# A two-level Winograd MLP on one core: one SBUF pool placed by a search over buffer times, w1 in quarter blocks, layer norm of the second half on two engines

## The chip, the core and the metric

The kernel runs on one core of a Trainium2 chip. The core has a matrix engine (TensorE, PE in the profile, with its weight loads as PEld), VectorE (DVE), ScalarE (ACT), GpSimd (POOL) and SyncE (SP), which here issues nearly all DMA transfers. Each engine executes its own instructions in order and waits for others through semaphores; SP's DMA instructions wait in the same way, so one that waits holds up those behind it. The metric is the device time of one execution in microseconds (us), as the median of several runs.

## The reference

```python
def _layernorm(x, axis=-1, eps=1e-5):
    m = jnp.mean(x, axis=axis, keepdims=True)
    v = jnp.var(x, axis=axis, keepdims=True)
    return (x - m) / jnp.sqrt(v + eps)

# x: 1 x 2048 x 1024, w1: 1024 x 3584, w2: 3584 x 1024, all bf16
def reference(x, w1, b1, w2, b2):
    y = _layernorm(x, axis=-1)
    h = _gelu(jnp.einsum("bsd,df->bsf", y, w1) + b1)
    return jnp.einsum("bsf,fd->bsd", h, w2) + b2
```

## The kernel before

**The two GEMMs.** The 2048 rows of x are two blocks of 1024 (b = 0, 1). Both GEMMs use Winograd's form of Strassen's algorithm, in which a 2 x 2 product of blocks takes 7 products instead of 8. The first GEMM has one level of it: an output group (b, r), r = 0 to 13, is computed in 7 *steps* q = 1 to 7 of 4 matmuls with 512 columns each (L880). Its operands are w1, in chunks of two groups, with four sums of each chunk (DVE, L747), and the normalized, transposed x (y) with three T sums (DVE, L696). The second GEMM has two levels: 7 outer products p, each for both blocks, each of 7 steps of 14 matmuls with 256 columns (L1133). Its operands are the gelu output h (A11 to A22, and their sums S1 to S4, L1048), inner sums of those (L1037), and "units" of W2: for product p and step q a unit of 448 KB is loaded by `w2_unit` from W2 itself (for q = 1, 2, 4 where the operand of p is a plain block of W2), from the scratch tensor w2_raw (q = 1, 2, 4 of the operands T1 to T4) or from w2_scr (the inner sums, q = 5, 6, 7, 3).

**Preparing W2.** Class `W2Sums` makes these scratch tensors while the first GEMM runs. It does so in slices of the 7 row tiles (0-2, 2-4, 4-6, 6-7), each of 14 lambdas in a row: loads of the blocks of W2 (L920), outer differences (L930), inner differences (L946), stores to w2_raw (L942) and w2_scr (L954). In each slice the sums of B11, which product 1 uses, come first, and those of T4, which product 4 uses, last. The temporaries lie in an allocator of their own, MZ, over a zone of 20 KB per partition at the end of the SBUF pool; buffers born before the first unit may not lie there.

**Around a group.** Class `Wino` combines the steps of a group in PSUM: ACT saves partial sums and copies banks (L806, L815), DVE adds (L823), ACT applies gelu (L799) in the first GEMM; in the second, DVE adds and finishes (L1065, L1078) and SP stores the output (L1057). Layer norm of a tile i of 128 rows is `norm(i)`: for tiles in `ACT_LN`, mean and variance by two ACT passes (L618, L621), else by two bn_stats and an aggregate on DVE (L635 to L638); then a power on POOL and the normalization on DVE. Tiles 8 to 15 (block 1) are all in `ACT_LN`. Their transposition is a DMA (L678).

**The order.** The program is written as a list of steps, `flat`. The opening and part of group rows 0 to 10 of block 0 lie ahead of it. Then come 53 steps for what is left of rows 0 to 10, 20 for rows 11 to 13, 98 for block 1 (from position `fB` = 73 on) and the steps of the second GEMM (from `fC` = 171 on), where a step of a group alternates with one of the group before. `put(i, f)` hangs other work on a position of this list. Such a position is the earliest one for DMAs: a load may not start before the PE step ahead of that position has ended (`gate`). A2_LA, A1_LA and UNIT_LA say how many steps ahead of its first use a load is placed, SUM_LA the same for the w1 sums, `W2_AT` from where to where a slice of W2 is spread ("A" counts from 0, "B" from fB), Y1_AT and Y1_STEP where the x tiles of block 1 go. Within these limits a list scheduler (`Program._simulate`) sets the order of instructions on each engine, by a latest start time (`alap`) that follows from the first PE step that needs the result. It runs on modelled durations: the PE order is fixed.

**The placement.** A first pass runs without limits of memory and gives each buffer a time of first use and of last use. Class `Plan` then gives each buffer its offset, largest area first, at the spot with the least lateness (`_pack`). The program is built again with these offsets; a buffer laid over an earlier one waits for that one's last users. This is repeated 6 times with learned times, and the order with the shortest modelled span is used.

**Sizes.** In bytes per partition, one h buffer (`h_unit`) has 7,168, and there are 4 x 2 of them in each block; a W2 unit has 3,584, a quarter of a w1 chunk 2,048, S1 of block 0 is 14,336 for itself.

## Time and profile before

| | us |
|---|---|
| runs of the kernel before, lowest / median / highest | 354.06 / 356.14 / 358.99 |
| the profiled execution | 357.63 |
| its span, first to last instruction | 355.9 |

The span is 1.7 us shorter than the profiled execution's own time. Times in profile rows are microseconds unless marked ns, counted from the start of the span. A row of a group of instructions has line, engine, operation, tiles, form and count, then busy time and mean ns of one, then the idle time of the engine ahead of them and what ended it. The last slices of the page's table of busy tenths belong to the second GEMM, which begins at about 190 us. The granted clock is the share of its full clock at which TensorE runs; 1.00 is full.

### The profile page before, as it was taken

How to read it: one execution, taken by the hardware profiler on the slowest of the kernel's cores; microseconds unless marked ns; L12 is line 12 of the kernel's file. 1: busy time of each engine (PE TensorE's matmuls, PEld its weight loads, DVE VectorE, ACT ScalarE, POOL GpSimd, SP SyncE). 2: the span in 40 equal slices, each digit the busy share in tenths (PEclk: the TensorE clock that was granted, in tenths of full speed). 3: DMA queues.
4: the chain of work that ended last, by engine and by line, in shares of the span. 5: the costliest groups of instructions: out<-in, count | busy, mean ns of one | idle time of the engine just before them, and what ended most of it. 6: DMA issues, size and time to landing. Idle time of an engine off the chain costs nothing.

```text
span 355.9 us, 6022 instructions
## 1 busy us (share of the span) xinstructions
PE 336.5 (95%) x2363; PEld 221.4 (62%) x2363; DVE 294.6 (83%) x465; ACT 187.2 (53%) x327; POOL 13.3 (4%) x32
## 2 busy tenths in 40 slices
PE   8899999979979999998996999999999999998995
PEld 6754443434424444443443778888888888886884
DVE  5976599986989769777999899969997897797964
ACT  2498999979957676674765433353111112211110
POOL 2210101001300000000000000000000000000000
PEclk9999999999999999999999899999999999999999
DMA  7961988999997799879996355373665737558552
GB/s 242 320 150 29 290 277 307 235 331 320 225 294 213 225 334 291 253 249 316 278 287 191 103 152 161 104 207 119 190 183 157 206 116 199 171 176 236 162 159 64
DMA packets 99157, 75.82 MB, mean 213 GB/s; under 512 B 11962, under 2 KB 90426, under 8 KB 99130
## 3 DMA queue, kind: packets, MB, share of 16 engines
q1 hardware_dynamic: 98986, 75.32, 72.0%
q8 instruction: 18, 0.29, 0.4%
q10 hardware_dynamic: 144, 0.13, 0.1%
q14 instruction: 9, 0.07, 0.1%
HBM read 48.96 MB, written 24.38 MB: 206 GB/s over the span
## 4 chain that ended last, share of the span: by engine, by line
PE 62%; DMA 23%; ACT 6%; DVE 5%; issue 3%; SPq 1%; DVEq 0%
PE ps L1133 34%; PE ps L880 26%; DMA mem<-in_w_dram 10%; DMA mem<-w_raw 7%; DMA mem<-in_x_dram 5%; ACT mem L799 2%; DVE mem L747 2%; ACT mem L815 2%; PE ps L1184 2%; DMA mem<-w_scr 1%; DVE ps L823 1%; PE ps L664 1%; DVE mem L946 1%; ACT mem L621 1%; DVE mem L696 1%
## 5 line engine op out<-in xcount | busy, mean ns | idle before, releaser
L880 PE MATMUL ps<-mem 128*128 128x512 f16 x756 | 167.6, 381 | 6.7 <-ACT mem L815 2.6
L1133 PE MATMUL ps<-mem 128*128 128x256 f16 (+1 forms) x1372 | 152.7, 273 | 7.3 <-DMA mem<-w_raw 4.2
L1133 PEld LDWEIGHTS ps<-mem 128*128 128x128 f16 x1372 | 133.8, 98 | 26.8 <-DMA mem<-w_raw 5.9
L880 PEld LDWEIGHTS ps<-mem 128*128 128x128 f16 (+1 forms) x756 | 72.5, 98 | 98.1 <-ACT mem L815 6.6
L815 ACT COPY mem<-ps 128x512 f32<-128x512 f32 x111 | 65.5, 595 | 82.4 <-PE ps L1133 69.9
L799 ACT ACTIVATE mem<-ps,b_sb 128x512 f16<-128x512 f32 x112 | 74.2, 705 | 22.7 <-DVE ps L823 13.6
L823 DVE TENSOR_TENSOR ps<-ps,mem 128x512 f32<-128x512 f32 x84 | 58.2, 693 | 19.1 <-ACT mem L815 14.2
L1037 DVE TENSOR_TENSOR mem<-mem 128x1792 f16<-128x1792 f16 x56 | 60.0, 1084 | 8.7 <-PE ps L1133 6.2
L946 DVE TENSOR_TENSOR mem<-mem 128x512 f16<-128x512 bf16 (+5 forms) x84 | 38.1, 464 | 10.5 <-DMA w_scr<-mem 6.9
L747 DVE TENSOR_TENSOR mem<-mem 128x1024 f16<-128x1024 bf16 (+1 forms) x56 | 37.0, 686 | 6.5 <-DMA mem<-in_w_dram 6.2
L806 ACT COPY ps<-ps 128x512 f32<-128x512 f32 x31 | 17.9, 576 | 34.7 <-PE ps L1133 31.0
L1048 DVE TENSOR_TENSOR mem<-mem 128x1792 f16<-128x1792 f16 x32 | 34.0, 1082 | 1.9 <-PE ps L1133 1.9
L1065 DVE TENSOR_TENSOR mem<-ps,mem 128x512 bf16<-128x512 f32 x24 | 16.3, 684 | 3.7 <-DMA out_dram<-mem 2.0
L930 DVE TENSOR_TENSOR mem<-mem 128x2048 f16<-128x2048 bf16 (+1 forms) x16 | 17.4, 1087 | 0.2
L1078 DVE TENSOR_TENSOR mem<-ps,mem 128x512 f32<-128x512 f32 x24 | 16.1, 682 | 1.2 <-PE ps L1133 1.1
L635 DVE BATCH_NORM_STATS2 st_sb<-mem 128x6 f32<-128x512 bf16 x16 | 10.4, 671 | 5.0 <-DMA mem<-in_x_dram 5.0
L669 ACT COPY mem<-ps 128x512 f16<-128x512 f16 x16 | 8.7, 604 | 10.2 <-PE ps L664 10.2
L696 DVE TENSOR_TENSOR mem<-mem 128x512 f16<-128x512 f16 x32 | 12.0, 418 | 0.2
L618 ACT ACTIVATE mem<-mem 128x1024 f16<-128x1024 bf16 x8 | 8.6, 1072 | 2.8 <-DMA mem<-in_x_dram 2.7
L621 ACT ACTIVATE mem<-mem,mv_sb 128x1024 f16<-128x1024 bf16 x8 | 9.4, 1172 | 0.0
L1154 PE MATMUL ps<-ones 128*128 128x128 bf16 (+1 forms) x58 | 7.6, 307 | 1.0 <-POOL nhalf L585 1.0
L1184 PE MATMUL ps<-mem 128*128 128x128 f16 x112 | 7.6, 219 | 0.3 <-ACT mem L669 0.2
(30 smaller groups left out, 70.9 us busy)
## 6 DMA issues: line engine op xcount, KB each, us to landing
mem<-in_w_dram SPq DMA_DIRECT2D x52, 256.0 KB, 5.3
mem<-w_scr SPq DMA_DIRECT2D x28, 448.0 KB, 3.4
w_scr<-mem SPq DMA_DIRECT2D x21, 512.0 KB, 4.7
mem<-in_w_dram SPq DMA_DIRECT2D x14, 512.0 KB, 5.0
w_raw<-mem SPq DMA_DIRECT2D x12, 512.0 KB, 4.3
mem<-w_raw SPq DMA_DIRECT2D x12, 448.0 KB, 4.5
out_dram<-mem SPq DMA_DIRECT2D x32, 128.0 KB, 2.9
mem<-in_w_dram SPq DMA_DIRECT2D x9, 448.0 KB, 4.0
```

The lines of the kernel that those rows point to most:

```text
L747: op("DVE", d_tt(n), lambda e: e.tensor_tensor(out=o[0], in0=a[0], in1=bb[0], op=f), r=[a[1], bb[1]], w=[o[1]], name=f"w1S{k}_{ch}")
L799: op("ACT", A_GELU, lambda e: e.activation(out=dst, in_=bank2(bank), func=ACT.Gelu_apprx_tanh, bias=b1_sb[:, f:f + 1], scale=1.0), r=[bank ...
L806: op("ACT", A_CP, lambda e: e.copy(out=banks[dst][:, :], in_=banks[src][:, :]), r=[bank_c[src]], w=[bank_c[dst]], name=name, lat=A_LAT)
L815: op("ACT", A_CP, lambda e: e.copy(out=v16(a, 0, 2048, F32), in_=banks[src][:, :]), r=[bank_c[src]], w=[a.c()], name=name, lat=A_LAT)
L823: op("DVE", D_PS, lambda e: e.tensor_tensor(out=banks[dst][:, :], in0=banks[src][:, :], in1=v16(a, 0, 2048, F32), op=ALU.add), r=[bank_c[s ...
L880: i = e.matmul(banks[bank][:, :], lhsT=lv[:, k, :], rhs=rv[:, k, :], start=(fresh and k == 0), stop=(k == KH - 1), skip_group_check=True)
L930: op("DVE", d_tt(2 * self.n), lambda e: e.tensor_tensor(out=vd, in0=va, in1=vb, op=ALU.subtract), r=self.cells(a) + self.cells(bb), w=self ...
L946: tt = lambda o, a, c: (lambda e: e.tensor_tensor(out=o, in0=a, in1=c, op=ALU.subtract))
L1037: op("DVE", d_tt(UN // 2), lambda e: e.tensor_tensor(out=v16(t), in0=a[0], in1=bb[0], op=f), r=a[1] + bb[1], w=[t.c()], name=f"in{b}_{p}{q}")
L1048: op("DVE", d_tt(UN // 2), lambda e, va=va, vb=vb, vd=vd: e.tensor_tensor(out=vd, in0=va, in1=vb, op=f), r=h_cells(b, a, u, s) + h_cells(b ...
L1065: op("DVE", D_PS, lambda e: e.tensor_tensor(out=v16(o, 0, 1024, BF16), in0=a, in1=bb, op=ALU.add), r=[na, nb], w=[o.c()], name=name, lat=D ...
L1133: i = e.matmul(bank2(bank)[:, t, :], lhsT=av3[:, k, t * P:(t + 1) * P], rhs=bv[:, k, :], start=(fresh and t == 0 and k == 0), stop=(t == 1 ...
```

## The change

1. **One pool.** MZ and its zone go. The W2 temporaries are allocated from M, as all other buffers.
2. **The search.** `pack` places the buffers once, largest first, and then for 4000 rounds takes a few of them out and puts them back elsewhere, keeping what lowers a total. The total counts, for each two buffers that share bytes one after the other, how much the later one would wait, and 0.02 of what is missing to 25 us between the last use of the one and the first of the other. One round instead of 6, with a fixed seed.
3. **The planner's model.** DMA instructions take 0.6 us to issue instead of 0.5, DMA transposes 2.0; short-run transfers go at 0.27 MB/us instead of 0.36. Work may be given a due time: `due(f, 20)` bounds the finish of what f emits to 20 us after the PE step ahead of its position. The steps of `W2Sums` have it, and norm, transposition and T sums of block 1.
4. **w1 in quarters.** Each half of A1 and of A2 is a buffer and a load of 256 KB of its own; A2 was one load of 512 KB. The quarters are freed one by one.
5. **Positions.** In block 1 w1 is loaded 12 steps ahead instead of 8 and summed 7 ahead instead of 6; in block 0 the 12 and 6 stay. Units are loaded 4 steps ahead for the first product and 5 for the others, instead of 3; inner sums of h 5 ahead instead of 6. The slices of W2 are spread wider. Tiles of x in block 1 follow each other by 6 steps instead of 3.
6. **Layer norm of block 1.** Tiles 8, 10, 12, 14 keep their statistics on ACT; 9, 11, 13, 15 have theirs on DVE.
7. **Order of the outer products.** 1, 4, 2, ... instead of 4, 1, 2, ...; h sums that follow a product's last plain use are placed at its step q = 4 instead of behind its last step.

```diff
-SLACK = 4.0
-ZONE = 20 * 1024 - 192
-DMA_ISSUE = 0.5
-PACK_ROUNDS = 6
+SLACK = 25.0
+Z_LATE = 3.0
+DMA_ISSUE = 0.6
+PREFER = 0.02
+PACK_ITERS = 4000
+DMA_SHORT, DMA_LONG = 0.27e6, 0.36e6
+PACK_ROUNDS = 1
...
+        slack = np.where(first, t0[None, :] - t1[:, None], t0[:, None] - t1[None, :])
+        late = np.maximum(0.0, WAR - slack) + PREFER * np.maximum(0.0, SLACK - slack)
+        late = np.round(late * 64) / 64
+        late[live] = 0.0
...
+        for it in range(PACK_ITERS):
+            if total <= 0.01:
+                break
+            i = rng.choices(ids, weights=costs + 1e-3 * total / m)[0]
...
+            if new.sum() / 2 <= total + 0.02 * rng.random() * total * (1 - it / PACK_ITERS):
+                costs, total = new, new.sum() / 2
+            else:
+                self.off = was
...
-                t.alap = fin - t.lat - t.dur * 1.3 - 0.1 - t.eager
+                if t.due is not None:
+                    fin = min(fin, t.due[0].at + t.due[1])
+                t.alap = fin - t.lat - t.dur * 1.3 - 0.1
...
-                        issue = DMA_ISSUE
+                        issue = 2.0 if t.name[:2] == "Td" else DMA_ISSUE
...
-P_ORDER = (4, 1, 2, 6, 7, 5, 3)
-A1_LA, A2_LA, SUM_LA = 8, 8, 6
+P_ORDER = (1, 4, 2, 6, 7, 5, 3)
+A1_LA, A2_LA, SUM_LA = (12, 12), (12, 12), (6, 7)
...
-ACT_LN = (8, 9, 10, 11, 12, 13, 14, 15)
-UNIT_LA, IN_LA = 3, 6
-W2_AT = ((0, 2, ("A", 2), ("A", 34)), (2, 4, ("A", 36), ("A", 68)), (4, 6, ("B", -6), ("B", 28)), (6, 7, ("B", 30), ("B", 60)))
+ACT_LN = (8, 10, 12, 14)
+UNIT_LA, IN_LA = (4, 5), 5
+W2_AT = ((0, 2, ("A", 2), ("A", 40)), (2, 4, ("A", 40), ("B", 16)), (4, 6, ("B", 16), ("B", 50)), (6, 7, ("B", 50), ("B", 75)))
...
+DUE_Y = 20.0
+DUE_W = 20.0
...
-Y1_AT, Y1_STEP = -6, 3
+Y1_AT, Y1_STEP = -6, 6
...
+                i = int(which[1]) - 1
+                o = i * FH + ch * 256
+                for h in range(2):
+                    bf = W[b, ch, f"{i + 1}{h + 1}"] = M.alloc(KH * 512, f"w1{i}{h}_{b}{ch}")
+                    dma("SP", lambda e, h=h, bf=bf: e.dma_start(v3(bf, 0, KH * 512, KH, BF16), w1v[:, h * KH:(h + 1) * KH, o:o + 256]),
+                        [], [bf.c()], P * KH * 512, None, f"w1{i}{h}_{b}{ch}")
...
-                    bf = self.B[nm] = MZ.alloc(4 * self.n, nm)
+                    bf = self.B[nm] = M.alloc(4 * self.n, "z" + nm)
...
-                            put(first_use((b, rows[0]), (1, 2, 5, 6, 7)) - A1_LA - 4, lambda ch=ch: w1_load(0, ch, "A1"))
+                            put(first_use((b, rows[0]), (1, 2, 5, 6, 7)) - A1_LA[0], lambda ch=ch: w1_load(0, ch, "A1"))
...
-                put(y1at + Y1_STEP * (i - 8) + 3, lambda i=i: (norm(i), to_yT_dma(1, i)))
-            put(y1at + 8 * Y1_STEP + 3, lambda: (t_new(1), tsum(1, 0), tsum(1, 1)))
-            put(y1at + 8 * Y1_STEP + 5, lambda: (tsum(1, 2), tsum(1, 3)))
+                put(y1at + Y1_STEP * (i - 8) + 3, due(lambda i=i: (norm(i), to_yT_dma(1, i)), DUE_Y))
+            for t in range(4):
+                put(y1at + (t + 5) * Y1_STEP + 6, due(lambda t=t: ((t_new(1) if t == 0 else None), tsum(1, t)), DUE_Y))
...
-                spread(W2Sums(k0, k1).steps(), pos(lo), pos(hi))
-            put(pos(W2_AT[-1][3]), lambda: M.inherit(MZ))
+                spread([due(f, DUE_W) for f in W2Sums(k0, k1).steps()], pos(lo), pos(hi))
...
-                lb = {p: last_use(("c", b, p)) for p in P_ORDER}
+                lb = {p: first_use(("c", b, p), (4,)) for p in P_ORDER}
...
-                    put(i - UNIT_LA, lambda p=p, q=q: w2_unit(p, q))
+                    put(i - (UNIT_LA[0] if p == P_ORDER[0] else UNIT_LA[1]), lambda p=p, q=q: w2_unit(p, q))
```

More of the change, by code (lines that the diff above doesn't have):

```diff
@@ L30 @@
 class Buf:
-    __slots__ = ("off", "n", "cells", "prior", "name", "born", "gone", "t0", "t1", "early")
+    __slots__ = ("off", "n", "cells", "prior", "name", "born", "gone", "t0", "t1", "late")
     def __init__(self, off, n, prior, name):
@@ L251, in free @@
         self.past.append((b.off, b.off + b.n, list(dict.fromkeys(tasks))))
-    def inherit(self, mem):
-        assert not mem.live
-        self.past += [(o, e, tasks) for o, e, _, tasks in mem.past]
 class Task:
     __slots__ = ("i", "eng", "dur", "lat", "fn", "deps", "succ", "name", "start", "end", "done", "alap", "sem", "val", "clock",
-                 "nsig", "at", "eager")
+                 "nsig", "at", "due")
     def __init__(self, i, eng, dur, lat, fn, name):
@@ L594, in dma @@
                     extra = tuple(extra) + (gate[0],)
-                return op(q, nbytes / 0.36e6, fn, r=r, w=w, name=name, sem=sem, extra=extra)
+                short = name[:2] in ("w1", "ld", "st") or (name[0] == "u" and name[2] in "123")
+                return op(q, nbytes / (DMA_SHORT if short else DMA_LONG), fn, r=r, w=w, name=name, sem=sem, extra=extra)
             xb = {}
```

260 lines of the change are left out of this document (115 added, 145 removed).

## The prediction

> **What bounds the kernel now.** I read the page first, then the busy time by stages, then the chain of work that ended last, then what TensorE waited for.
>
> ```profile
> span 355.9 us, 6022 instructions
> ```
> ```profile
> PE 336.5 (95%) x2363; PEld 221.4 (62%) x2363; DVE 294.6 (83%) x465; ACT 187.2 (53%) x327; POOL 13.3 (4%) x32
> ```
>
> TensorE (PE) is busy 95% of the span, so only its losses can be won. I count them by stage: the length of a stage less its matmuls at full pace. The pace comes from two unbroken stretches of the chain (start, us, what):
>
> ```profile
> 105.08 53.72 PE ps L880 x248
> ...
> 258.38 17.00 PE ps L1133 x154
> ```
>
> That is 53.72/248 = 0.2166 us for a 512-column matmul of the first GEMM and 17.00/154 = 0.1104 us for a 256-column one of the second. One step of the written-out order is 4 of the former (0.87 us) or 14 of the latter (1.55 us). The stages (columns: stretch, length, then busy us and count of PE, PEld, DVE, ACT, POOL, then granted clock, DMA share, GB/s):
>
> ```profile
> 40.00:105.00 65.00, 59.77 (x271) 25.22 (x269) 56.60 (x99) 59.09 (x107) 7.66 (x16) 1.00 1.01 287
> 105.00:190.00 85.00, 83.40 (x384) 37.34 (x384) 70.69 (x132) 58.29 (x97) 0.00 (x0) 1.00 0.86 267
> 190.00:203.00 13.00, 10.11 (x67) 7.16 (x68) 11.41 (x12) 5.40 (x10) 0.00 (x0) 0.87 0.52 157
> 203.00:353.00 150.00, 145.51 (x1319) 128.02 (x1316) 127.61 (x158) 37.41 (x65) 0.00 (x0) 1.00 0.57 164
> ```
>
> Stage A, 40 to 105, loses 65 - 271 x 0.2166 = 6.3 us. Stage B, 105 to 190: 85 - 384 x 0.2166 = 1.8. The entry of the second GEMM, 190 to 203, holds 56 matmuls of L1133 and 11 of L880 (timeline below): 13 - 6.2 - 2.4 = 4.4. Stage C, 203 to 353: 150 - 1319 x 0.1104 = 4.4. Together 16.9 us; no change of order or placement can win more. What PE waited for (us in total, times, longest):
>
> ```profile
> PE ps L1133 <- DMA mem<-w_raw: 4.2, 4, 3.0
> PE ps L880 <- ACT mem L815: 2.6, 3, 2.0
> PE ps L880 <- DMA mem<-in_w_dram: 2.0, 2, 1.0
> PE ps L1133 <- DMA mem<-in_w_dram: 1.9, 2, 1.7
> PE ps L880 <- DVE mem L696: 1.4, 1, 1.4
> ...
> PE ps L1133 <- ACT mem L815: 0.7, 1, 0.7
> ```
>
> The entry, on PE (start, us, what, [idle before <- releaser]):
>
> ```profile
> 186.73 3.19 PE L880 MATMUL ps<-mem 128*128 128x512 f16 x14
> 192.89 1.95 PE L1133 MATMUL ps<-mem 128*128 128x256 f16 x14 [2.97 <-DMA mem<-w_raw]
> 194.63 1.91 PE L880 MATMUL ps<-mem 128*128 128x512 f16 x4
> 196.34 3.85 PE L1133 MATMUL ps<-mem 128*128 128x256 f16 x28
> 200.03 1.03 PE L880 MATMUL ps<-mem 128*128 128x512 f16 x4
> 200.89 1.69 PE L1133 MATMUL ps<-mem 128*128 128x256 f16 x14
> 202.42 0.81 PE L880 MATMUL ps<-mem 128*128 128x512 f16 x3
> ```
>
> The first W2 unit lands too late and PE idles 2.97 us. Behind that the clock falls: four matmuls take 1.91 us where four take 1.03 later. The granted clock of 0.87 over these 13 us is 1.7 us more.
>
> **The change part by part.** Sums are made against the profiled execution: 357.6 us, its span 355.9 and 1.7 around it. It lies 1.5 above the median, 356.1; I take that off at the end.
>
> **LN of block 1 on two engines.** Four of eight tiles leave ACT. The groups concerned (busy us, mean ns of one), with those of the W2 preparation:
>
> ```profile
> L946 DVE TENSOR_TENSOR mem<-mem 128x512 f16<-128x512 bf16 (+5 forms) x84 | 38.1, 464 | 10.5 <-DMA w_scr<-mem 6.9
> ...
> L930 DVE TENSOR_TENSOR mem<-mem 128x2048 f16<-128x2048 bf16 (+1 forms) x16 | 17.4, 1087 | 0.2
> ...
> L635 DVE BATCH_NORM_STATS2 st_sb<-mem 128x6 f32<-128x512 bf16 x16 | 10.4, 671 | 5.0 <-DMA mem<-in_x_dram 5.0
> ...
> L618 ACT ACTIVATE mem<-mem 128x1024 f16<-128x1024 bf16 x8 | 8.6, 1072 | 2.8 <-DMA mem<-in_x_dram 2.7
> L621 ACT ACTIVATE mem<-mem,mv_sb 128x1024 f16<-128x1024 bf16 x8 | 9.4, 1172 | 0.0
> ```
>
> ACT loses 4 x (1.07 + 1.17) = 9.0 us and falls from 59.1 to 50 of stage A's 65. DVE gains 4 x 2 x 0.671 = 5.4 us of statistics and some small ones, 6 in all, and would stand at 62.6 of 65 if nothing else left the stage. What can leave is the W2 preparation, of which stage A holds now (length, DVE busy us and count of L946 and of L930):
>
> ```profile
> 40.00:105.00 65.00, 13.57 (x27) 1.00 1.01 287
> ```
> ```profile
> 40.00:105.00 65.00, 8.55 (x7) 1.00 1.01 287
> ```
>
> That is 22.1 of 38.1 + 17.4 = 55.5 us. By the new positions the first slice (2/7 of it) ends at step 40 and the second (2/7) runs from step 40 to 89; stage A has 73 steps. Done by position, 48% or 26.5 us falls in stage A; done as late as the due time of 20 us (23 steps) lets it, 34% or 19.1. DVE then holds 59.6 to 67 of 65 us: nearly full, while ACT has air. Of the 6.3 us lost, 2.6 + 1.4 are in the rows of L815 and L696 and 1.0 is w1; the rest is pauses too short to be waits, and refill of the pipeline. I take 3.4 as won and 2.9 left. Bounds: all 6.3 won, or 2.0 (67 - 65) lost on top.
>
> The x loads go out every 6 steps instead of 3, the last at step 36 instead of 15; the T sums at 30 to 48, due 20 us on, so by step 71 of 73: ahead of block 1 by the plan's own clock. Late next would be w1.
>
> **w1 in quarters, asked for 12 steps ahead in block 1 instead of 8** (block 0's 12 stay). The 14 A2 loads of 512 KB become 28 of 256 KB. Issues (count, KB each, median us to landing):
>
> ```profile
> mem<-in_w_dram SPq DMA_DIRECT2D x52, 256.0 KB, 5.3
> ...
> mem<-in_w_dram SPq DMA_DIRECT2D x14, 512.0 KB, 5.0
> ...
> mem<-in_w_dram SPq DMA_DIRECT2D x9, 448.0 KB, 4.0
> ```
>
> A half lands no sooner than a whole, 5.3 against 5.0; 12 x 0.87 = 10.4 us of lookahead cover it, and SP's 14 more issues. I take 0 for the split. Below nothing it goes only by freeing SBUF, counted with the placement; above, see the last rival. [...] Stage B's loss was w1 arriving late and its sums behind it:
>
> ```profile
> 159.15 5.78 DMA mem<-in_w_dram
> ```
>
> I leave 0.6 of 1.8, so 1.2 is won. Bounds: all of it; or nothing, if these loads wait for a buffer and not for their position.
>
> **Entry: product 1 first, units 4 steps ahead instead of 3, W2 temporaries in the common pool.** Product 4 needs T4, the last W2 step, through w_raw; product 1's operand is W2 itself, and its sums are made early in each slice. The last slice ends at step 75 of stage B's 98 instead of 60, plus at most 23 for the due time; T4 has 14 more steps to land. Four steps of 0.87 before PE's end at 189.92 is an issue at 186.5; with 4.0 us (the 448 KB row) the unit lands at 190.5, 0.6 us of idle instead of 2.97. But SBUF is fullest here: h of both blocks holds 114.7 KB of a partition, S1 14.3 more, while y, T and w1 of the last rows still live, and A22 is freed one product later. I take 1.5 left of 4.4, the clock not falling: 2.9 won. Bounds 3.9 and 0.
>
> **Stage C: units 5 steps ahead.** Its waits are the tails of unit loads, the longest of them
>
> ```profile
> 318.98 6.25 DMA mem<-in_w_dram
> ```
>
> against 3 x 1.55 = 4.6; five steps are 7.7 us and cover it. Left is the final drain, 0.7 by the L815 row, and 0.5 of others: 1.2 of 4.4, 3.2 won. Bounds 3.7 and 0.
>
> **The placement.** The search charges every reuse of a buffer closer than 25 us, but the pool is full at the entry and units live longer. No row prices a new wait. Below nothing it cannot go: the waits that it could remove are counted above. Above, one unit as late as at the entry, 2.97 + 1.7 = 4.7. I take 0.6, near the short waits that most of the rows show. The opening keeps its order: 0, give or take 0.5. Issue times and bandwidths in the planner's model change the order alone.
>
> Sum: 3.4 + 1.2 + 2.9 + 3.2 - 0.6 = 10.1. 357.6 - 10.1 = 347.5, and at the median 1.5 less: 346.0 us.
>
> **The rivals.** *DVE takes ACT's place in stage A.* For it: 59.6 to 67 of 65 us, in order, so that one late statistic delays the L823 addition on which a gelu waits. Against it: the W2 sums may slip 20 us. Stage A then loses its 6.3 and some 0.6 of the bound's 2.0 instead of 2.9: 346.0 + 4.0 = 350.
>
> *The reuse of buffers at the entry and for w1 stays what it was.* For it: the fullness there. Then 2.9 + 1.2 of the gain is missing and the 0.6 is not paid: 349.5. It leaves a stall of 2 to 3 us at the entry. In this trace 2.97 us of idle brought the lower clock; 2.0 us in stage A (the L815 row) did not, as the clock there is 1.00. [...]
>
> *Slower: late unit buffers.* Two more units of 3.6 KB live at once in a full pool. A unit whose buffer is freed only by the step before its use stalls PE for its whole landing, 4.0 us, and for 1.7 of clock: 5.7. Two of these eat the gain, from three on it is slower: 346.0 + 3 x 5.7 = 363. Against it: the longest stall in stage C now is 1.7, and the search avoids just this.
>
> *The split costs DMA time.* Against it the two rows. For it a DMA share of 1.01 in stage A. w1 stays late in A and B and x behind it: 1.0 + 1.2 + 3.4 of the gain goes: 351.6.
>
> **How the numbers follow.** Forecast 0.60, its own range 341 to 349.5; DVE 0.16; reuse unchanged 0.13; late units 0.09; split 0.02. Two per cent is 7.1 us, about what a measurement of this kernel can tell from no change: 349.0 and 363.3. Faster takes 0.57 of the forecast's 0.60 and 0.06 of the two rivals near 350; slower takes 0.07 of the late units; the rest, 0.30, lies within. The range, 341 to 353, leaves out 0.05 of the forecast below, and above it the late units and some 0.05 of the others.
>
> **What would show it.** Right: L880's wait for L815 gone, and DVE above 59 us in the 65 before block 1; no wait of L880 for in_w_dram between 100 and 190; less than 2 us of idle before the first L1133 matmul, and clock 1.00 there; no wait of L1133 for a DMA above 0.5 in stage C. Wrong: unit loads of SP released by a matmul just before their use (late buffers); L823 or L747 ending PE's waits in stage A (DVE); 256 KB loads landing after 7 us (split).

## The result

| | before | changed |
|---|---|---|
| median of the runs, us | 356.09 | 340.21 |
| lowest and highest, us | 354.06, 358.99 | 339.84, 341.03 |
| profiled execution, its span, us | 357.63, 355.9 | 339.84, 338.0 |

The ratio is 0.9551 with a 95% interval of 0.9482 to 0.9621: 4.5% faster. (A fourth run of the kernel before, 356.04 us, moves its median from 356.14 to 356.09.) The forecast was 346.0 us, with a range of 341 to 353. The direction was right, the gain was 15.9 us instead of 10.1, and the time lies 0.8 us below the range.

The page of the changed kernel:

```profile
span 338.0 us, 6056 instructions
```
```profile
PE 331.9 (98%) x2363; PEld 222.0 (66%) x2363; DVE 295.3 (87%) x481; ACT 179.4 (53%) x311; POOL 15.2 (5%) x28
```

PE is now busy 98% of the span; DVE has 16 instructions more and ACT 16 less (the layer norm). Everything that PE waited for (us in total, times, longest):

```profile
PE ps L1145 <- POOL nhalf L605: 1.0, 1, 1.0
PE ps L871 <- DVE mem L751: 0.8, 1, 0.8
PE ps L1124 <- ACT mem L806: 0.7, 1, 0.7
PE ps L1175 <- ACT mem L690: 0.2, 1, 0.2
PE ps L871 <- ACT ps L797: 0.2, 1, 0.2
```

Line numbers moved: L871 and L1124 are the matmuls that were L880 and L1133, L751 the w1 sums that were L747, L806, L797 and L842 the ACT copies that were L815, L806 and L851, L814 the additions on DVE that were L823, L921 and L937 the W2 differences that were L930 and L946, L639 and L642 the layer norm passes on ACT that were L618 and L621. No wait for a DMA is left in this list, where the kernel before had 8.5 us of them. The same from the chain of work that ended last, in which the two GEMMs are two long pieces, with six short ones of PE alone between them:

```profile
86.39 95.14 PE ps L871 x440
...
190.37 140.62 PE ps L1124 x1288
```

From 86.39 to 331.0 PE is not stopped. The pieces also give a better pace than the prediction had: 140.62/1288 = 0.1092 us for a 256-column matmul (it had 0.1104) and 95.14/440 = 0.2162 for a 512-column one.

The stages, as the prediction cut them (stretch, length, busy us and count of PE, PEld, DVE, ACT, POOL, granted clock, DMA share, GB/s):

```profile
40.00:105.00 65.00, 63.98 (x296) 28.29 (x294) 64.34 (x125) 53.56 (x96) 9.21 (x11) 1.00 1.09 307
105.00:190.00 85.00, 85.00 (x423) 41.09 (x422) 72.65 (x125) 58.73 (x98) 0.00 (x0) 1.00 0.85 273
190.00:203.00 13.00, 13.00 (x120) 11.56 (x119) 12.11 (x14) 6.10 (x12) 0.00 (x0) 1.00 0.68 192
```

In the first, DVE is busy 64.3 of 65 us: the engine that took over half of ACT's layer norm is full. Still PE does 296 matmuls there instead of 271.

For the comparisons below I use one measure: what PE lost in a stage. It is the sum, over that stage's matmuls, of the time to the start of the next one less that of a matmul at full pace: 0.2163 us (512 columns), 0.1092 (256) or 0.056 (128, the median spacing), worked out from the traces. A stage is bounded by matmuls, not by time: A runs from the first 512-column matmul of the first GEMM to the start of the first step of block 1, B to the last matmul ahead of the second GEMM, the entry from there, with the wait for the first W2 unit, to the last 512-column one, C is the rest. A value of -0.2 means a pace a little above that.

| lost by PE, us | opening | A | B | entry | C | sum |
|---|---|---|---|---|---|---|
| before | 4.9 | 5.3 | 3.2 | 4.8 | 5.7 | 23.9 |
| changed | 3.6 | 1.6 | -0.2 | 0.1 | 0.8 | 5.9 |
| difference | 1.3 | 3.7 | 3.4 | 4.7 | 4.9 | 18.0 |
| predicted difference | 0 | 3.4 | 1.2 | 2.9 | 3.2 | 10.7, less 0.6 for new waits |

The prediction's A reached some 3 us into B, with the wait for the T sums; A and B together gained 7.1 us where it had 4.6. But for rounding, the differences sum to the 17.9 us between the two spans. In the medians the gain is 2 us less, since the profiled execution before lay 1.5 above its median and the one of the changed kernel 0.4 below.

### The profile page after: what moved, and what is told of

It reads as the page before. It is cut to its first block, busy times and chain, and to the rows that moved or that the text cites. A ratio compares the mean times of both kernels' runs of the same rounds, so it can differ in the third digit from the quotient of the medians.

```text
span 338.0 us, 6056 instructions
## 1 busy us (share of the span) xinstructions
PE 331.9 (98%) x2363; PEld 222.0 (66%) x2363; DVE 295.3 (87%) x481; ACT 179.4 (53%) x311; POOL 15.2 (5%) x28
## 4 chain that ended last, share of the span: by engine, by line
PE 85%; DVE 9%; DMA 2%; issue 2%; POOL 0%; ACT 0%; DVEq 0%
PE ps L1124 44%; PE ps L871 37%; DVE ps L814 2%; PE ps L1175 2%; DVE mem L751 2%; DVE mem L937 2%; DVE st_sb L656 2%; DMA mem<-in_w_dram 1%; PE ps L685 1%; DMA mem<-in_x_dram 1%; DVE mem L717 1%; POOL rstd_sb L662 0%; DVE mem L664 0%; DVE mem L1056 0%; DVE mem L651 0%
## 5 line engine op out<-in xcount | busy, mean ns | idle before, releaser
L871 PE MATMUL ps<-mem 128*128 128x512 f16 x756 | 165.4, 379 | 1.0 <-DVE mem L751 0.8
L1124 PE MATMUL ps<-mem 128*128 128x256 f16 (+1 forms) x1372 | 150.6, 273 | 0.7 <-ACT mem L806 0.7
L1124 PEld LDWEIGHTS ps<-mem 128*128 128x128 f16 x1372 | 134.1, 98 | 17.5 <-ACT mem L806 1.0
L871 PEld LDWEIGHTS ps<-mem 128*128 128x128 f16 (+1 forms) x756 | 73.2, 98 | 89.8 <-DVE mem L751 2.2
L806 ACT COPY mem<-ps 128x512 f32<-128x512 f32 x111 | 65.0, 593 | 82.3 <-PE ps L1124 67.3
L790 ACT ACTIVATE mem<-ps,b_sb 128x512 f16<-128x512 f32 x112 | 73.3, 696 | 26.1 <-PE ps L871 15.6
L814 DVE TENSOR_TENSOR ps<-ps,mem 128x512 f32<-128x512 f32 x84 | 58.3, 695 | 23.8 <-ACT mem L806 21.8
L751 DVE TENSOR_TENSOR mem<-mem 128x1024 f16<-128x1024 bf16 (+1 forms) x56 | 37.5, 685 | 0.6 <-DMA mem<-in_w_dram 0.2
L937 DVE TENSOR_TENSOR mem<-mem 128x512 f16<-128x512 f16 (+5 forms) x84 | 37.4, 463 | 0.7 <-DMA mem<-in_w_dram 0.4
L797 ACT COPY ps<-ps 128x512 f32<-128x512 f32 x31 | 17.7, 572 | 26.5 <-PE ps L1124 20.4
L656 DVE BATCH_NORM_STATS2 st_sb<-mem 128x6 f32<-128x512 bf16 x24 | 15.6, 675 | 6.0 <-DMA mem<-in_x_dram 5.9
L921 DVE TENSOR_TENSOR mem<-mem 128x2048 f16<-128x2048 bf16 (+1 forms) x16 | 17.3, 1083 | 0.0
L717 DVE TENSOR_TENSOR mem<-mem 128x512 f16<-128x512 f16 x32 | 12.2, 418 | 0.1
L662 POOL TENSOR_TENSOR rstd_sb<-vpe_sb,nhalf 128x1 f32<-128x1 f32 x12 | 7.9, 663 | 50.2 <-DVE vpe_sb L659 50.2
L664 DVE TENSOR_SCALAR mem<-mem,mv_sb,rstd_sb 128x1024 f16<-128x1024 bf16 x12 | 6.3, 536 | 0.8 <-POOL rstd_sb L662 0.7
```

Source lines behind the costliest of these rows:

```text
L656: op("DVE", 0.62, lambda e, i=i, h=h: e.bn_stats(st_sb[:, i, 6 * h:6 * (h + 1)], v16(b, h * D, D, BF16)), r=[b.c(h)], w=[c_st[i][h]], name ...
L751: op("DVE", d_tt(n), lambda e: e.tensor_tensor(out=o[0], in0=a[0], in1=bb[0], op=f), r=[a[1], bb[1]], w=[o[1]], name=f"w1S{k}_{ch}")
L790: op("ACT", A_GELU, lambda e: e.activation(out=dst, in_=bank2(bank), func=ACT.Gelu_apprx_tanh, bias=b1_sb[:, f:f + 1], scale=1.0), r=[bank ...
L797: op("ACT", A_CP, lambda e: e.copy(out=banks[dst][:, :], in_=banks[src][:, :]), r=[bank_c[src]], w=[bank_c[dst]], name=name, lat=A_LAT)
L806: op("ACT", A_CP, lambda e: e.copy(out=v16(a, 0, 2048, F32), in_=banks[src][:, :]), r=[bank_c[src]], w=[a.c()], name=name, lat=A_LAT)
L814: op("DVE", D_PS, lambda e: e.tensor_tensor(out=banks[dst][:, :], in0=banks[src][:, :], in1=v16(a, 0, 2048, F32), op=ALU.add), r=[bank_c[s ...
```

## The experiments

In each the stated edit was made to the changed kernel, or to the kernel before where that is said. One caution holds for most of them: an edit that changes positions or buffers makes the planner place all buffers and order all instructions anew, so that the trace differs in other places too; what one such run adds to the time is then not the price of its edit alone. In runs 9, 10, 13 and 14 the offsets were therefore pinned to those of the changed kernel, and only the final order was made under another rule. The last column but one is the ratio to runs of the kernel before on the same chip.

| run | edit | us | ratio, 95% interval | lost: opening, A, B, entry, C |
|---|---|---|---|---|
| changed | | 340.21 | 0.9551 (0.948 to 0.962) | 3.6, 1.6, -0.2, 0.1, 0.8 |
| 1 | no local search | 343.98 | 0.9629 (0.958 to 0.967) | 3.7, 3.3, -0.2, 1.0, 1.0 |
| 2 | units 3 steps ahead | 352.78 | 0.9883 (0.983 to 0.994) | 3.7, 8.0, -0.2, 1.6, 5.1 |
| 3 | layer norm on ACT alone | 345.58 | 0.9674 (0.963 to 0.972) | 3.6, 5.7, -0.2, 0.9, 0.8 |
| 4 | old DMA figures | 348.44 | 0.9750 (0.971 to 0.980) | 4.5, 5.0, 4.0, 0.9, 0.8 |
| 5 | seed 0 | 347.12 | 0.9717 (0.966 to 0.977) | 3.9, 7.9, -0.2, 1.1, 0.8 |
| 6 | seed 1 | 346.48 | 0.9701 (0.965 to 0.976) | 3.9, 1.6, 5.4, 1.2, 0.8 |
| 7 | A2 of w1 whole | 341.12 | 0.9543 (0.948 to 0.961) | 3.8, 4.0, -0.2, 0.1, 0.8 |
| 8 | product 4 first | 349.04 | 0.9770 (0.971 to 0.983) | 3.7, 8.9, -0.2, 1.3, 0.8 |
| 9 | pinned, old DMA figures | 347.61 | 0.9698 (0.964 to 0.976) | 4.3, 5.1, 2.6, 1.4, 0.8 |
| 10 | pinned, no due times | 341.64 | 0.9527 (0.947 to 0.958) | 3.7, 0.5, 0.4, 1.4, 0.8 |
| 11 | W2 slices later, seed 2 | 340.58 | 0.9506 (0.944 to 0.957) | 3.6, 0.9, 0.2, 1.2, 0.8 |
| 12 | W2 slices later, seed 0 | 341.24 | 0.9527 (0.947 to 0.959) | 3.7, 2.3, 0.0, 1.0, 0.8 |
| 13 | pinned, old bandwidth | 346.03 | 0.9695 (0.964 to 0.975) | 4.6, 4.5, 1.8, 0.8, 0.8 |
| 14 | pinned, old transpose time | 340.34 | 0.9531 (0.947 to 0.959) | 4.0, 1.6, -0.1, 1.1, 0.8 |
| 15 | before, new DMA figures | 368.66 | 1.0328 (1.026 to 1.039) | 4.3, 1.6, 2.3, 17.8, 4.6 |
| 16 | before, layer norm on both | 368.61 | 1.0309 (1.024 to 1.038) | 4.5, 3.8, 18.5, 1.9, 6.2 |
| 17 | W2 slices later, seed 1 | 340.08 | 0.9525 (0.949 to 0.956) | 4.1, 0.6, -0.2, 1.0, 0.8 |
| 18 | changed, again | 340.50 | 0.9544 (0.950 to 0.959) | 3.4, 1.1, -0.2, 0.9, 0.8 |

The lost time is that of one profiled execution each.

### Run 1: no local search

```diff
-PACK_ITERS = 4000
+PACK_ITERS = 0
```

> The changed kernel with the local search left out: offsets from the first greedy pass alone, everything else as changed. If the offsets carry the gain (buffer reuse was what made unit and w1 loads late), waits for loads of W2 units and w1 come back and the time is 348 to 354 us. If the positions carry it (units 4 and 5 steps ahead, w1 12 steps ahead), the time stays at 340 to 343 us and no wait of TensorE for a load exceeds 1 us.

Measured 343.98 us, between the two expectations. Beside the changed kernel's ratio the loss is 0.8%, some 3 us, with intervals that just overlap: 1.7 more in A, and one wait of 1.9 us for an ACT copy there is the longest. No wait for a load exceeds 0.8 us.

```profile
PE ps L871 <- ACT ps L842: 1.9, 1, 1.9
...
PE ps L1124 <- DMA mem<-in_w_dram: 0.8, 1, 0.8
```

So the 4000 rounds of the search are not what removed the late loads. What its greedy pass has in common with the search, one pool and a charge on reuse closer than 25 us, is in both.

### Run 2: units 3 steps ahead

```diff
-UNIT_LA, IN_LA = (4, 5), 5
+UNIT_LA, IN_LA = (3, 3), 5
```

> The changed kernel with W2 units loaded 3 steps ahead again. If the lookahead carries the second GEMM's gain, the waits of TensorE for unit loads come back: 1 to 2 us at the entry and 3.5 us in stage C, 344.5 to 346 us. If the units were late because of their buffers, the time stays within 1.5 us of 340.2 and no unit wait in stage C exceeds 0.5 us.

Measured 352.78 us. Stage C and the entry behave as the first theory says: 4.3 us come back in C and 1.5 at the entry (0.7 beside run 18's 0.9), as waits for unit loads (in_w_dram and w_raw below). The rest of the 12 us lies in A: one w1 load waited on for 4.8 us, in an execution with a mean granted clock of 0.989, where run 18 has 1.0.

```profile
PE ps L871 <- DMA mem<-in_w_dram: 4.8, 1, 4.8
PE ps L1124 <- DMA mem<-in_w_dram: 3.3, 3, 1.5
...
PE ps L1124 <- DMA mem<-w_raw: 0.9, 2, 0.5
```

That stall lies 100 us ahead of the first unit. I put it down to the new placement and order, which the edit also drew, and not to the lookahead. It is the first sign of what runs 5 and 6 test.

### Run 3: layer norm of block 1 on ACT alone

```diff
-ACT_LN = (8, 10, 12, 14)
+ACT_LN = (8, 9, 10, 11, 12, 13, 14, 15)
```

> The changed kernel with the statistics of all eight tiles of block 1 on ACT. If ACT bound stage A, 3 to 4 us come back there as waits for the ACT copies, 343 to 344.5 us. If the spreading of the tiles (6 steps instead of 3) and the due times had already given ACT air, the time is 339.5 to 341.5 us; it would even be lower if DVE, at 64 of 65 us in stage A, was what lost the 1.6 us there.

Measured 345.58 us, 1.3% above the changed kernel by the ratios. Stage A loses 5.7 us instead of 1.6, in waits for ACT:

```profile
PE ps L871 <- ACT ps L842: 2.0, 3, 1.2
PE ps L871 <- DVE ps L814: 1.1, 1, 1.1
```

The waits are those of the first theory, the time lies above its range. In this run's chain of work the layer norm passes of ACT (L639, L642) stand again and again just ahead of the copies (L842) that PE waits for. So ACT does hold up stage A when it has all eight tiles, even at 6 steps from tile to tile; the amount is that of one new draw of placement and order.

### Run 4: the old figures for DMA in the planner's model

```diff
-DMA_ISSUE = 0.6
+DMA_ISSUE = 0.5
-DMA_SHORT, DMA_LONG = 0.27e6, 0.36e6
+DMA_SHORT, DMA_LONG = 0.36e6, 0.36e6
-                        issue = 2.0 if t.name[:2] == "Td" else DMA_ISSUE
+                        issue = DMA_ISSUE
```

> The changed kernel planned with the old figures for DMA (issue 0.5 us, one bandwidth, transposes as other DMAs). If the opening's gain comes from the order that these figures give on DVE (normalization of tile 1 ahead of the statistics of tile 2), the opening loses 1.2 us again and the time is 341.5 us or more, with whatever the wrong transpose time costs in stage A (0 to 3 us). If that order is the same, or the gain there was the chance of one execution, the opening keeps its start of 17.0 us for the first 512-column matmul and the time stays within 1 us of 340.2.

Measured 348.44 us, 2% above the changed kernel by the ratios: more than the expectation's opening and stage A. 0.9 us is the opening, 3.4 stage A, and 4.2 stage B, where the expectation had nothing. These figures touch no instruction; the kernel only comes out in another order, and with other buffer times for the search. Runs 9, 13 and 14 separate the two.

### Runs 5 and 6: other seeds

```diff
-SEED = 2
+SEED = 0
```

(run 6: `SEED = 1`)

> The changed kernel with another seed of the search (0 instead of 2); nothing else differs. If the search clears the reuse waits whatever its start, the time stays within 1.5 us of the changed kernel's 340.2 to 341.4 and TensorE's losses stay under 4 us from 20 us on. If the placement is a lottery of which one ticket was kept, some w1 or unit load waits for its buffer again and the time is 344 us or more, with a single wait of 2 to 5 us in the trace.

> As the run before, with seed 1. Reliable search: 340 to 342.5 us. Lottery: 344 us or more. The two seeds and the greedy placement (344.0 us) together tell whether the gain over the greedy placement is the search's or the seed's.

Measured 347.12 and 346.48 us. The second theory holds in the time and in the single long wait: the search is a lottery at these positions. But what PE waits for is a w1 sum on DVE, not a load. Each of the two seeds loses 6 to 7 us by one stall, of 4.0 us in A (run 5) and 3.7 in B (run 6), and by the medians is slower than the greedy placement of run 1 (the intervals of the ratios overlap a little). In run 5 the stall stands out in the stages and in DVE's order of time:

```profile
87.00:92.00 5.00, 1.00 (x6) 0.41 (x5) 5.00 (x11) 1.27 (x2) 0.00 (x0) 1.00 1.22 284
92.00:100.00 8.00, 8.00 (x31) 3.28 (x30) 6.83 (x14) 3.81 (x6) 0.00 (x0) 0.79 0.95 295
```
```profile
88.77 0.69 DVE L814 TENSOR_TENSOR ps<-ps,mem 128x512 f32<-128x512 f32 x1
89.37 1.21 DVE L921 TENSOR_TENSOR mem<-mem 128x2048 f16<-128x2048 bf16 x1
90.50 1.89 DVE L751 TENSOR_TENSOR mem<-mem 128x1024 f16<-128x1024 bf16 x3
```

While PE stands still, DVE is busy 5.00 of 5 us. PE waits for a w1 sum (L751), and ahead of it in DVE's queue an outer difference of W2 (L921, 1.21 us) is executed, for a GEMM that begins 100 us later. That one instruction is 1.2 of the 4.0 us. The rest is a queue that stands ahead of it: from 76 us on DVE's rows have no idle time, with W2 differences (L937), T sums (L717) and layer norm between the additions and the w1 sums. The next 8 us have a granted clock of 0.79.

### Run 7: A2 of w1 as one load

```diff
+                if i == 1:
+                    bf = W[b, ch, "21"] = W[b, ch, "22"] = M.alloc(KD * 512, f"w1b{b}{ch}")
+                    dma("SP", lambda e, bf=bf: e.dma_start(v3(bf, 0, KD * 512, KD, BF16), w1v[:, :, o:o + 256]),
+                        [], [bf.c(0), bf.c(1)], P * KD * 512, None, f"w1b{b}{ch}")
+                    return
```

(its users read at an offset, and both halves are freed together)

> The changed kernel with A2 of w1 as one buffer and one load of 512 KB again; A1 stays in halves. If halves cost DMA time (a fixed part per transfer), this is faster by up to 2 us in stage A, 338.5 to 340 us. If the split is worth its freed SBUF, buffer waits come back: 342 to 346 us. If it does neither, 340 to 341.5 us; the landing times of 256 and 512 KB are then again within 0.5 us of each other.

Measured 341.12 us, the same as the changed kernel by the ratios: the third expectation. Halves and wholes land within 0.3 us of each other here (5.6 and 5.9):

```profile
mem<-in_w_dram SPq DMA_DIRECT2D x52, 256.0 KB, 5.6
...
mem<-in_w_dram SPq DMA_DIRECT2D x14, 512.0 KB, 5.9
```

The split of w1 neither costs nor gives time at these positions. The A stage's 4.0 us in the table is from a profiled execution of 343.09 us, the longest of this kernel's runs, with a stall of 2.16 us from 55.0 us on and a granted clock of 0.89 from 50 to 60 us and of 0.93 from 60 to 70.

### Run 8: product 4 ahead of product 1

```diff
-P_ORDER = (1, 4, 2, 6, 7, 5, 3)
+P_ORDER = (4, 1, 2, 6, 7, 5, 3)
```

> The changed kernel with product 4 ahead of product 1 again. If the order of the products set the entry (T4 comes last of the W2 work, and its last slice now ends 13 us later than before), the first unit from w_raw or the first from w_scr is late by 2 to 6 us, half clock included: 343 to 348 us. If the step of lookahead and the due time of 20 us are enough for it, the entry loses under 1 us more and the time is 340 to 342 us.

Measured 349.04 us, but not where the first theory put it. The entry loses 1.3 us, 0.4 more than in run 18, so the order of the products is worth little once the W2 sums are early (the last W2 difference starts at 172.0 us here, 18 us ahead of the second GEMM). The other 7 us are one stall in A again, a wait of 6.4 us for a w1 sum:

```profile
PE ps L871 <- DVE mem L751: 6.4, 1, 6.4
PE ps L1124 <- DMA mem<-w_raw: 1.2, 1, 1.2
```

### Runs 9, 13 and 14: offsets pinned, old figures in the final order

```diff
+            DMA_ISSUE, DMA_SHORT, TD_ISSUE = 0.5, 0.36e6, 0.5
             got.schedule(T_PE)
```

(run 13: `DMA_SHORT = 0.36e6` alone; run 14: `TD_ISSUE = 0.6` alone)

> The offsets of the changed kernel, but the order of the instructions set with the old figures for DMA (issue 0.5, one bandwidth, transposes like other DMAs). So only order differs. If the order that the new figures give is part of the gain, the opening loses some 1 us again and stage A, where DVE has 0.8 us to spare of 65, loses 1 to 4 more: 342 to 346 us. If the offsets alone carry it, 340 to 341.5 us.

> Offsets of the changed kernel; of the planner's figures for DMA only the bandwidth of short-run transfers is the old one (0.36 instead of 0.27 MB/us). If this figure is what the order was worth, DVE again stands in its queue before w1 sums whose loads have not landed (10.0 us of waits of L751 for in_w_dram with all old figures, 0.2 in the changed kernel), and the time is 344 to 348 us. If not, those waits stay under 2 us and the time under 342.5.

> Offsets of the changed kernel; of the planner's figures only the issue time of the transposes is the old one (as any DMA, 0.6 instead of 2.0 us). If this figure carries the order's 6 us, 344 to 348 us, with the loss in stage A alone, where the transposes are. If the bandwidth figure carries it, under 342.5 us.

Measured 347.61, 346.03 and 340.34 us. The offsets are the same in all three, so the order alone is worth 5 us or more, and it is the bandwidth figure that makes it; the transposes' issue time makes no difference (340.34, ratio within the interval of the changed kernel). What DVE waited for shows why. The kernel before, the changed one, and run 13:

```profile
DVE mem L946 <- DMA w_scr<-mem: 6.9, 6, 3.3
...
DVE mem L747 <- DMA mem<-in_w_dram: 6.2, 10, 1.6
...
DVE mem L946 <- DMA mem<-in_w_dram: 2.8, 3, 1.3
```
```profile
DVE mem L937 <- DMA mem<-in_w_dram: 0.4, 2, 0.3
...
DVE mem L751 <- DMA mem<-in_w_dram: 0.2, 1, 0.2
```
```profile
DVE mem L751 <- DMA mem<-in_w_dram: 8.6, 8, 3.0
```

With 0.36 MB/us the planner expects loads in short runs sooner than with 0.27, and puts the sums that use them early in DVE's queue. DVE then stands before them, 8.6 us in all, with the additions (L814) behind them on which ACT and PE wait. With 0.27 these waits are 0.2 us. The longest stall of run 13 shows it, on DVE, on ACT and on PE:

```profile
52.75 0.69 DVE L751 TENSOR_TENSOR mem<-mem 128x1024 f16<-128x1024 bf16 x1 [1.29 <-DMA mem<-in_w_dram]
...
55.61 0.69 DVE L814 TENSOR_TENSOR ps<-ps,mem 128x512 f32<-128x512 f32 x1
```
```profile
56.34 1.27 ACT L790 ACTIVATE mem<-ps,b_sb 128x512 f16<-128x512 f32 x2 [1.62 <-DVE ps L814]
...
58.55 0.58 ACT L842 COPY ps<-mem 128x512 f32<-128x512 f32 x1
```
```profile
59.19 7.19 PE L871 MATMUL ps<-mem 128*128 128x512 f16 x32 [1.68 <-ACT ps L842]
```

Not every such wait reaches PE: in run 17 the w1 sums wait 5.1 us for their loads, and PE loses 0.6 us in A and nothing in B.

The kernel before is less clear than its rows above suggest. The 6.9 us are differences that wait for a store to w_scr to leave a buffer that they write again, and stores to w_scr are not among the transfers whose figure changed. And its longest stall in stage A came by ACT's own queue, in which a layer norm pass waited for its x tile, with the copy behind it:

```profile
74.86 1.06 ACT L618 ACTIVATE mem<-mem 128x1024 f16<-128x1024 bf16 x1 [2.11 <-DMA mem<-in_x_dram]
...
75.92 0.56 ACT L815 COPY mem<-ps 128x512 f32<-128x512 f32 x1
```
```profile
76.54 7.94 PE L880 MATMUL ps<-mem 128*128 128x512 f16 x36 [2.03 <-ACT mem L815]
```

The opening is the same in small. In the kernel before the normalization of tile 1 stood behind statistics that waited 1.49 us for their tile:

```profile
9.58 0.69 DVE L635 BATCH_NORM_STATS2 st_sb<-mem 128x6 f32<-128x512 bf16 x1 [1.49 <-DMA mem<-in_x_dram]
10.19 0.53 DVE L643 TENSOR_SCALAR mem<-mem,mv_sb,rstd_sb 128x1024 f16<-128x1024 bf16 x1
```

In the changed kernel it stands ahead of them, and runs at 8.12:

```profile
8.12 0.49 DVE L664 TENSOR_SCALAR mem<-mem,mv_sb,rstd_sb 128x1024 f16<-128x1024 bf16 x1
...
9.28 1.28 DVE L656 BATCH_NORM_STATS2 st_sb<-mem 128x6 f32<-128x512 bf16 x2 [0.61 <-DMA mem<-in_x_dram]
```

In run 13 it is behind them again, and the opening loses 1.0 us more than in the changed kernel.

### Run 10: offsets pinned, no due times in the final order

```diff
+            for t in got.tasks:
+                t.due = None
             got.schedule(T_PE)
```

> The offsets of the changed kernel, but the final order is set without due times. If the due times matter, the W2 sums and T sums slip as before and the waits return at the start of block 1 (2 to 3 us) and at the entry of the second GEMM (w_scr or w_raw, 1 to 4 us): 343 to 347 us. If the wider positions and the placement do it, 339.5 to 341.5 us; with W2 work slipping out of stage A, DVE would even have air there and lose less than the 1.5 us.

Measured 341.64 us, ratio 0.9527: the same as the changed kernel. With the placement made, the due times are not needed; A and B together lose 0.9 us, as in run 18, and the entry 1.4.

### Runs 11, 12 and 17: W2 slices later, three seeds

```diff
-W2_AT = ((0, 2, ("A", 2), ("A", 40)), (2, 4, ("A", 40), ("B", 16)), (4, 6, ("B", 16), ("B", 50)), (6, 7, ("B", 50), ("B", 75)))
+W2_AT = ((0, 2, ("A", 2), ("A", 52)), (2, 4, ("A", 52), ("B", 28)), (4, 6, ("B", 28), ("B", 58)), (6, 7, ("B", 58), ("B", 78)))
```

(seeds 2, 0 and 1)

> The changed kernel with the W2 slices 10 to 12 steps later (2 to 52, 52 to block 1's 28, 28 to 58, 58 to 78), seed 2 as it was. If the full DVE in stage A is what is left there and what makes the other seeds lose 4 to 6 us, DVE has 3 us or more to spare in stage A and TensorE loses under 1 us there: 338.5 to 340.5 us. If it is the luck of the placement, this is a new draw: 341 to 347 us with one single wait of 2 to 5 us.

> As the run before with seed 0, which lost 7 us with the slices as they were. Full DVE as the cause: 338.5 to 341 us again, so that the seed no longer matters. Luck of the placement: a third draw, 341 to 347 us.

> The later W2 slices (2 to 52, 52 to block 1's 28, 28 to 58, 58 to 78) with seed 1, which lost 6 us in block 1 with the slices as they were. If a full DVE in stage A is what lets one late load show, 338.5 to 342 us, within 0.4% of the changed kernel beside it. If placement is the cause, another single wait of 2 to 5 us, 343 us or more.

Measured 340.58, 341.24 and 340.08 us. The seed no longer matters: seeds 0 and 1 lost 6 to 7 us before, and here all three end within 1.2 us. But the reason given was wrong in one point. DVE has no more air than before: it is busy 53.4 of the 54 us from 38 to 92 in run 17, and 53.7 in the changed kernel timed beside it (run 18).

```profile
38.00:92.00 54.00, 53.68 (x249) 23.97 (x248) 53.44 (x108) 48.06 (x86) 9.30 (x12) 1.00 1.07 292
```
```profile
38.00:92.00 54.00, 53.18 (x247) 23.77 (x246) 53.68 (x107) 47.32 (x85) 8.88 (x12) 1.00 1.13 309
```

A full engine does not show how much work stands in its queue, though. W2 differences (L921 and L937) hold 15.9 us of this stretch in run 17 and 18.6 in run 18, and in run 17 additions, w1 sums and T sums fill the difference. With later positions, and with them later due times, W2 work is less urgent and does not stand ahead of a w1 sum; whether its smaller amount or its place in the queue counts, these runs do not part. Run 10, where the due times alone are gone, speaks for the place. That this is what cured seeds 0 and 1 rests on run 5's order and on the absence of any stall beyond 1.7 us in three draws; the placement was also drawn anew.

### Run 15: the kernel before with the new DMA figures

```diff
-DMA_ISSUE = 0.5
+DMA_ISSUE = 0.6
...
+                short = name[:2] in ("w1", "ld", "st") or (name[0] == "u" and name[2] in "123")
+                return op(q, nbytes / (0.27e6 if short else 0.36e6), fn, r=r, w=w, name=name, sem=sem, extra=extra)
...
+                        issue = 2.0 if t.name[:2] == "Td" else DMA_ISSUE
```

> The kernel before with the new figures for DMA alone; placement, positions and layer norm are the old ones. If the order alone is worth some 6 us, DVE's waits for in_w_dram and w_scr (6.2, 2.8 and 6.9 us) shrink and the time falls by 3 to 6 us, to 352 to 355 on a chip where the kernel before takes 358. If the order pays only once loads are early and buffers free, the change is within 2 us either way.

Measured 368.66 us, 3.3% slower than before. Neither expectation held. Stage A loses 1.6 instead of 5.3 us, as much as in the changed kernel, so the new order pays there, within a new placement. It does so without the shrinking that was expected: DVE's waits for w1 loads are 5.9 us instead of 6.2, those for w_scr 5.0 instead of 6.9, and only those of the W2 differences for loads go, from 2.8 to 0.3. What is gone is ACT's wait for x tiles, 2.7 us in the kernel before.

```profile
DVE mem L748 <- DMA mem<-in_w_dram: 5.9, 10, 2.2
...
DVE mem L947 <- DMA w_scr<-mem: 5.0, 6, 2.7
```

But the entry loses 17.8: the first unit of product 4 from w_raw comes 14.61 us late, as the last W2 step was put off that far.

```profile
179.76 4.91 PE L881 MATMUL ps<-mem 128*128 128x512 f16 x22
199.28 3.17 PE L1134 MATMUL ps<-mem 128*128 128x256 f16 x14 [14.61 <-DMA mem<-w_raw]
```

### Run 16: the kernel before with four tiles of layer norm on DVE

```diff
-ACT_LN = (8, 9, 10, 11, 12, 13, 14, 15)
+ACT_LN = (8, 10, 12, 14)
```

> The kernel before with the statistics of four of the eight tiles on DVE, nothing else changed. By the prediction's term 3 to 4 us are won in stage A, where TensorE waited for ACT. If DVE, which stood there 8.4 us idle on loads and ACT copies, cannot take the 6 us as well, the gain is under 1.5 us or the sign turns.

Measured 368.61 us, 3.1% slower. Stage A loses 3.8 us instead of 5.3. Then, at the second step of block 1, the first that uses a T sum, PE waits 14.0 us:

```profile
PE ps L880 <- DVE mem L696: 14.0, 1, 14.0
```

In its chain of work an x tile of block 1 is loaded at 104.08 us only, behind a transposition, and its layer norm and T sums follow when PE already waits for them. The longest stall of stage A, 2.1 us, is again a copy on ACT behind a layer norm pass that waits for its x tile (2.45 us). Four tiles on DVE come with 1.5 us less in stage A here, 4 within the changed kernel (run 3), and the edit can cost more at the next deadline than it gives, unless positions or due times bring that work forward.

### Run 18: the changed kernel again

> The changed kernel as it is, for a paired time on this chip: 340 to 342 us. If the later W2 slices with seed 1 are within 1.5 us of it, the gain needs no particular seed.

Measured 340.50 us, beside 340.08 for run 17 on the same chip. Over the kernel before, 0.9544 and 0.9525, with overlapping intervals: no version among these is shown to be faster than the changed kernel.

## Why the prediction was right in its direction and too small in its size

**What bounds the kernel.** Right: only PE's losses could be won, and they were. Wrong: "16.9 us; no change of order or placement can win more". 17.9 us were won. Two things were left out of that ceiling. The opening was outside the stages, as if it could not change. And the pace of stage C came from 154 matmuls in 17.00 us, a stretch in which one matmul's whole 0.27 us counts; over 1288 matmuls it is 0.1092 instead of 0.1104, and stage C's loss by the prediction's own formula is 150 - 1319 x 0.1092 = 6.0 us instead of 4.4.

**The planner's figures: the step that failed.** The prediction said "Issue times and bandwidths in the planner's model change the order alone", and counted nothing. The order is worth 5.7 us by itself (346.03 us in run 13 against 340.34 in run 14, with offsets pinned): 0.6 in the opening, 2.9 in A and 1.9 in B. That run 13, with the old bandwidth figure, comes out at the forecast of 346.0 is chance, since the other terms were off as well. The profile of before had the kind of loss in view: DVE waited 6.2 and 2.8 us for loads, ACT 2.7 us for x tiles, in order, in front of work on which PE depended. I read what PE waited for, found ACT copies there, and did not read what ACT and DVE waited for. How much of the kernel before's own loss the old figures made stays open, since the one run on it (run 15) kept most of DVE's waits.

**Layer norm.** The mechanism is borne out in the changed kernel, where it is worth some 4.1 us in A by run 3 (one draw), against 3.4 that the prediction took for all of A. For the kernel before the prediction misread the row of L815: of its 2.6 us, 2.0 were not an ACT that has too much to do, but one that waited 2.11 us for an x tile. DVE at 64.3 us lies inside the predicted 59.6 to 67. DVE did become the full engine, and in this execution the chain of work runs almost wholly through it in the 34 us ahead of 86.39; it costs PE 1.6 us. The two causes do not add: with layer norm on ACT alone (run 3) A loses 5.7, with the old bandwidth figure (run 13) 4.5, in the kernel before, with neither, 5.3.

**w1.** Right that the split costs nothing (run 7: 0.9543 against 0.9551, landing after 5.9 us as a whole and 5.6 in halves). Stage B's loss went entirely, with the start of block 1; the 0.6 left in the forecast was not there.

**Entry.** Too small: 4.7 us instead of 2.9. I left 1.5 for the fullness of SBUF. The stall was 0.1 in this execution and 0.9 in run 18's, 0.6 by the working in the text before that allowance. The W2 sums are early now: the last difference starts at 168.0 us, 13.5 ahead of the second GEMM, where the kernel before had 187.7 and 5.2. With product 4 first the entry loses 1.3 (run 8), with units 3 steps ahead 1.6 (run 2), so neither the order of the products nor the lookahead alone made the 4.8. What is left is the earlier W2 sums, which no run took alone.

**Stage C.** Mechanism right (run 2: 4.3 us come back there), size 4.9 instead of 3.2: 1.3 of that is the pace (5.7 us were lost before, not 4.4), and of the 1.2 that I left 0.8 was there.

**The placement.** I took 0.6 us of new waits with a bound of 4.7. In the changed kernel there are none. Nor did I count what the one pool removes on DVE, 6.9 us of waits for w_scr (run 15, with the old zone, keeps 5.0); what they cost PE no run shows. At other seeds there is one stall of about 4 us with a lower granted clock (a mean of 0.994 in run 5 and 0.995 in run 6), 6 to 7 us in all, so that seeds 0 and 1 end at 347.1 and 346.5. The bound was the typical case, not the extreme. That the seed that was kept has no such stall is luck as far as the prediction goes: with either of the other two the same change comes out within the range. How much of the difference between seeds is reuse of buffers and how much is the order that follows from it stays open: no run held the order and changed the offsets alone.

**The rivals.** None took place in the changed kernel. *DVE takes ACT's place* shows its sign there, a wait of PE for a w1 sum (L751), but with 0.8 us only; it is what runs 5 and 8 show in full, by a mechanism that I had named only in half: a full DVE hurt where work that was not urgent stood ahead of a w1 sum (in run 5 an outer difference of 1.21 us, with a wait of 4.0 us on PE). *Late unit buffers*: in stage C of the changed kernel PE waits for no unit.

## What to carry to other kernels

Where an offline planner writes the order, its durations are part of the kernel: with short-run loads figured at 0.36 MB/us instead of 0.27, their consumers came earlier in DVE's queue, the w1 sums waited 8.6 us for them instead of 0.2 (run 13 and the changed kernel), and the time was 346.03 us instead of 340.21. So read the waits of the engine that feeds the matrix engine, and of the one that feeds that engine, and compare each modelled transfer time with its landing time in the profile. Take the pace for "what can be lost" from the longest unbroken stretch, count the opening in, and before a placement is credited with a gain, time it with two other seeds; a form of the schedule whose time does not depend on the seed, as in runs 11, 12 and 17, is the safer result.

## What the runs showed of the hardware

TensorE's granted clock was lower behind some of PE's waits and not behind others. In the kernel before it was 0.50 from 194.2 to 197.6 us, behind the wait of 2.97 us, and 1.00 in the 8 us behind the one of 2.03 us that ended at 76.54. In run 7, behind a wait of 2.16 us, 15 matmuls of 512 columns took 5.10 us, where the pace of 0.2162 gives 3.2; in run 16, behind one of 2.14 us, 20 took 4.49, nearly that pace, and in run 1 the clock was 1.00 behind one of 1.90 us. Run 7, then run 1 (the granted clock is the third number from the end):

```profile
50.00:60.00 10.00, 7.84 (x33) 3.17 (x31) 7.87 (x15) 7.65 (x14) 1.17 (x2) 0.89 1.10 293
60.00:70.00 10.00, 10.00 (x45) 4.39 (x44) 8.62 (x16) 8.19 (x15) 1.55 (x2) 0.93 1.00 276
```
```profile
70.00:80.00 10.00, 8.10 (x38) 3.54 (x37) 9.58 (x20) 8.08 (x15) 1.09 (x2) 1.00 1.06 314
```

The waits of 4.8, 4.0, 3.7 and 6.4 us in runs 2, 5, 6 and 8 all stand in executions with a lower mean clock: 0.989, 0.994, 0.995 and 0.990. With their spans of 350.3, 345.6, 345.0 and 346.6 us that is an estimate of 3.9, 2.1, 1.7 and 3.5 us lost to the clock in the whole execution. In runs 15 and 16, with waits of 14.6 and 14.0 us, the clock of 0.978 and 0.980 comes to 8.0 and 7.3 us in the same way; the ten 512-column matmuls behind the wait of run 16 took 4.45 us, twice what ten take at full pace (2.16). By these estimates the stall of 4.0 us in run 5 is one of 6.1, and that of 3.7 in run 6 one of 5.4, which is most of the 6 us by which the seeds differ.
